# A gated linear attention with a sorted mixture of experts on one core: column tiles for the gate loop's small matmuls, and expert tiles of 128 tokens with all weights held in SBUF

## The chip, the core and the metric

The kernel runs on one core of one Trainium2 chip, in one launch. The metric is the device time of that launch in microseconds. The engines are named as the profile names them: PE (TensorE matmuls), PEld (TensorE weight loads), DVE (VectorE), ACT (ScalarE), POOL (GpSimd) and SP (SyncE). SP issues only DMAs here. A name with a q behind it (SPq, POOLq) is the sequencer or queue of that engine.

## The reference

There are two parts, and the first one's output is the input of the second. The first is a recurrence over 768 positions for 4 x 8 heads with a state of 48 x 48 complex numbers:

```
for t in range(S):                              # S = 768, B = 4, H = 8, D = 48
    new_re = ar * S_re - ai * S_im              # ar, ai: the gate of step t, cut to |a| <= 0.999
    new_im = ar * S_im + ai * S_re
    S_re, S_im = new_re + outer(k[t], v[t]), new_im
    y[t] = q[t] @ S_re
```

The second takes the rows of y, one row of 8 x 48 = 384 numbers for each of the N = 3072 tokens, and sends each token to the best of 8 experts:

```
logits = x @ w_gate + modality_bias[modality_id]      # x: (3072, 384), 8 experts
e_idx  = argmax(logits);  gate_w = softmax(logits)[e_idx]
out[mask_e] = gate_w * (relu(x[mask_e] @ w1[e]) @ w2[e])   # w1: (8, 384, 1024), w2: (8, 1024, 384)
```

All inputs and the output are float32.

## The kernel before

**Gate loop.** The recurrence is computed in blocks of L = 96 positions. The work is cut into two rounds of two batches each. For each round `elem(r)` does the elementwise part: it walks backwards over 12 chunks of 8 positions, normalises the gates (lines 64 to 81), forms running products of them on DVE (lines 84 and 85), scales q and k with them (lines 98 to 101), writes the scaled k to DRAM as `kh` (line 102), and turns the scaled q around on PE into the tile `QT` (lines 106 and 107). `A` and `QT` live in the pool `qt` with one buffer each, so the second round's `QT` can be written only when the first round's units have read theirs.

`units(r)` then does the matmuls: eight blocks g, and in each two batches b, so 16 units a round and 32 in all. A unit loads `KW` (the block's scaled k) and `V`, turns k around into `KT` (line 139, 140), multiplies it with `QT` into the 96 x 96 block `W` per head (line 145, in PSUM as `wp`), masks it into the second half of `KW` (line 146), turns the carried state `Z` around (line 150), and forms the new state and the output in one PSUM tile `py` (lines 160 and 164, in pairs of heads whose results lie on partitions 0 to 63 and 64 to 127). The output yT is copied twice (lines 170, 171); the float32 copy is multiplied with the gate weights `wgp` into the logits `lg_ps` (line 173: four accumulating matmuls with 8 columns of weights each), the bf16 copy is turned around and written to DRAM as the rows `x_rows` (lines 176 to 180). After both batches the logits of the block are turned around (line 185) and put into `lg`. In float32 a matmul that is no transpose shows up as two instructions in the profile.

**Routing.** `moe_sorted` opens its own pools once those of the gate loop are closed. DVE adds the bias, finds the best expert of each token, and counts tokens by expert (lines 258 to 308). Two small matmuls give ranks and counts, a scan gives each expert's first slot tile, and 32 float32 matmuls (line 344) build the list that says which token sits in which slot (`inv`, then `idg` for reading rows and `ids` for writing them).

**Experts.** Tokens sit in slot tiles of 256, each of which belongs to one expert. `cast_weights`, called ahead of the gate loop, has written bf16 copies of all weights to DRAM (`w1b`, `w2b`) through 16 casting DMAs on POOL's queue. `slot_tile(i)` reads the tile's expert into a register of SP, loads that expert's w1 and w2 from the bf16 copies (three buffers), gathers twice 128 rows by indirect DMA, turns them around (line 367), multiplies with w1 (line 375), applies relu on DVE and ACT by turns, multiplies with w2 (line 384), scales, and scatters twice 128 rows to the output by indirect DMA on POOL's queue (line 390). The first 12 slot tiles always run. The other 7 are nested conditionals; in the profiled execution one of them ran.

The order of the instructions on each engine is set by the framework's scheduler, which goes by program order and its own idea of when operands are ready; it also adds every semaphore wait, and gives a pool's place in SBUF to a later pool once its tiles have been read.

Of the kernel before, what the change touches and what calls it, by code (L numbers as in the profile page):

```python
# [22 lines left out]
def gate_loop(nc, ctx, tc, cpool, ident, identb, q, k, v, a_re, a_im, wgp, x_rows, lg):  # L23
# [3 lines left out]
    L = 96  # L27
# [18 lines left out]
    nc.gpsimd.affine_select(mask[:], mask[:], pattern=[[1, L]], compare_op=Alu.is_ge, fill=0.0, base=0, channel_multiplier=-1)  # L46

# [62 lines left out]
    def units(r):  # L110
# [4 lines left out]
        for g in range(G):  # L115
# [12 lines left out]
            lg_ps = ps.tile([8, NB, L], F32, name="lg_ps", tag="lg")  # L128
            for b in range(NB):
# [5 lines left out]
                KT = un.tile([C, H, L], F32, name="KT")  # L135
                for h4 in range(0, H, 4):
# [3 lines left out]
                    nc.scalar.copy(KT[:, h4:h4 + 4], tp[:])  # L140
                for h4 in range(0, H, 4):
                    wp = ps.tile([L, 4, L], F32, name="wp", bufs=2)
                    for i in range(4):
                        p = (b * H + h4 + i) * G + g
                        nc.tensor.matmul(wp[:, i, :], KT[:, h4 + i, :], QT[:, p, :], start=True, stop=True)  # L145
                    nc.vector.tensor_tensor(KW[:, h4:h4 + 4, C:], wp[:], mask[:, None, :].broadcast_to([L, 4, L]), Alu.mult)  # L146
# [25 lines left out]
                for j in range(J):  # L172
                    nc.tensor.matmul(lg_ps[:, b, :], wgp[:, j, :], yT[:, j, :], start=(j == 0), stop=(j == J - 1))  # L173
# [7 lines left out]
            lgT = un.tile([8, NB, L], F32, name="lgT")  # L181
            nc.scalar.copy(lgT[:], lg_ps[:])
            lp = ps.tile([L, NB, 8], F32, name="tl", tag="tp", bufs=2)
            for b in range(NB):
                nc.tensor.transpose(lp[:, b, :], lgT[:, b, :], ident[:8, :8])
# [11 lines left out]
def cast_weights(nc, moe_w1, moe_w2):  # L197

    E, Dt, F = moe_w1.shape
    w1b = nc.dram_tensor("w1b", (E, 128, Dt // 128, F), BF16, kind="Internal").ap()  # L200
    w2b = nc.dram_tensor("w2b", (E, 128, F // 128, Dt), BF16, kind="Internal").ap()
    for e in range(E):
        nc.gpsimd.dma_start(out=w1b[e], in_=moe_w1[e].rearrange("(k p) f -> p k f", p=128))
        nc.gpsimd.dma_start(out=w2b[e], in_=moe_w2[e].rearrange("(c p) d -> p c d", p=128))
    return w1b, w2b


def moe_sorted(nc, ctx, tc, cpool, identb, lg, x_rows, w1b, w2b, moe_modality_id, moe_modality_bias, out):

    N, Dt = out.shape  # L210
    E = w1b.shape[0]
    F = w1b.shape[3]
# [4 lines left out]
    SL = 256  # L217
    NL = N // SL
    NS = NL + E - 1
    HS = SL // 128  # L220
    NH = NS * HS
    NF = F // 128

# [3 lines left out]

# [243 lines left out]
```

## Time and profile before

| | |
|---|---|
| time, median of 3 runs | 740.69 us (739.15 to 748.84) |
| time of the profiled execution | 740.69 us |
| its span, first to last instruction | 739.0 us |
| mean granted TensorE clock | 0.80 |
| PE busy | 409.7 us (55%) |
| PEld busy | 307.4 us (42%) |
| DVE busy | 377.1 us (51%) |
| ACT busy | 268.0 us (36%) |
| POOL busy | 72.1 us (10%) |
| bytes moved by DMA | 91.42 MB |
| read from HBM, written to HBM | 86.75 MB, 29.59 MB |

Busy time is given over the whole span, and no engine is busy for much more than half of it, since the stages have different limits. The view of busy time by stretch therefore has to be read stage by stage. A matmul's mean duration is its latency; how often one starts is seen from the start times in the timeline. A wait is put down to the engine or transfer that ended last before the instruction began. The granted clock is the share of TensorE's full speed that was granted in a stretch.

### The profile page before, as it was taken

Reading aid. Unit: us, or ns where it says so; the run is one execution under the profiler, and the core shown is the slowest. Engines: PE = TensorE matmul, PEld = TensorE weight load, DVE = VectorE, ACT = ScalarE, POOL = GpSimd, SP = SyncE. Lnnn points to the kernel's source line nnn. Section 1 sums busy time; section 2 is a strip of 40 time slices with the busy share of each in tenths; the row PEclk is TensorE's granted clock in tenths of the full one; section 3 lists DMA queues with packets and bytes.
Section 4 is the critical chain, followed back from the end, with each engine's and each line's share of the span. In section 5 each row is a group of like instructions: output and inputs, shape, how many; then the busy total and the mean of one; then the engine's idle time right before and its main releaser. Section 6 shows DMA issues by size and latency. Waiting matters only on the chain. (4 is left out here: it accounts for less than half of the span.)

```text
span 739.0 us, 8928 instructions
## 1 busy us (share of the span) xinstructions
PE 409.7 (55%) x3112; PEld 307.4 (42%) x3112; DVE 377.1 (51%) x838; ACT 268.0 (36%) x597; POOL 72.1 (10%) x112
## 2 busy tenths in 40 slices
PE   0111112128988888921111789999993578686724
PEld 0101101016766666620110566777772556464412
DVE  3877777761276567787777023333335414232201
ACT  2545454532355446764544223334331002121100
POOL 4110000000000000000000000000000043344231
PEclk9999999999699679965555556879787559898866
DMA  9999923243346253243230433334201627676320
GB/s 208 235 249 244 259 65 128 64 132 93 82 101 166 55 142 78 60 156 122 64 107 30 112 73 79 78 79 95 57 21 6 256 72 280 231 252 221 131 64 4
DMA packets 107953, 91.42 MB, mean 124 GB/s; under 512 B 72894, under 2 KB 96866, under 8 KB 107904
## 3 DMA queue, kind: packets, MB, share of 16 engines
q1 hardware_dynamic: 28512, 51.27, 21.5%
q0 software_dynamic: 14432, 19.86, 12.9%
q10 hardware_dynamic: 64960, 19.67, 11.8%
q8 instruction: 26, 0.43, 0.2%
q14 instruction: 23, 0.19, 0.1%
HBM read 86.75 MB, written 29.59 MB: 157 GB/s over the span
## 5 line engine op out<-in xcount | busy, mean ns | idle before, releaser
L106 PE MATMUL tq<-ident,Qh 128*96 128x128 f32 x192 | 41.9, 392 | 218.3 <-DVE Qh L100 216.6
L106 PEld LDWEIGHTS tq<-ident,Qh 128*96 128x96 f32 x192 | 31.6, 181 | 227.8 <-ACT g L75 176.8
L146 DVE TENSOR_TENSOR KW<-wp,mask 96x384 f32<-96x384 f32 x64 | 35.1, 553 | 120.2 <-PE wp L145 119.1
L160 PE MATMUL py<-KW,V 96*64 96x192 f32 x512 | 81.6, 401 | 7.7 <-issue 6.1
L84 DVE TENSOR_TENSOR x<-A,an 128x192 f32<-128x192 f32 x192 | 68.6, 357 | 31.1 <-ACT an L81 25.4
L145 PE MATMUL wp<-QT,KT 96*96 96x96 f32 x512 | 70.8, 302 | 1.5 <-ACT KT L140 1.4
L145 PEld LDWEIGHTS wp<-QT,KT 96*96 96x96 f32 x512 | 62.9, 210 | 10.8 <-ACT Zs L152 4.5
L379 ACT ACTIVATE hT<-h_ps 128x512 bf16<-128x512 f32 x26 | 15.5, 597 | 130.4 <-PE h_ps L375 77.4
L93 ACT ACTIVATE sqe<-A 128x768 f32<-128x768 f32 x24 | 20.2, 843 | 96.3 <-DVE A L85 96.3
L133 POOL MEMSET V<- 96x128 f32 x32 | 6.4, 212 | 475.9 <-PE py L160 351.6
L85 DVE TENSOR_TENSOR A<-x 128x96 f32<-128x96 f32 x192 | 49.4, 257 | 6.4
L375 PE MATMUL h_ps<-xgT,w1t 128*128 128x256 bf16 x312 | 47.3, 321 | 5.8 <-DVE xgT L368 4.5
L160 PEld LDWEIGHTS py<-KW,V 96*64 96x64 f32 x512 | 40.2, 165 | 19.6 <-issue 14.9
L164 PE MATMUL py<-QT,Zs 96*48 96x96 f32 x448 | 48.2, 281 | 0.0
L139 PE MATMUL tk<-ident,KW 96*96 96x96 f32 x256 | 39.8, 297 | 11.8 <-DMA KW<-kh 10.6
L375 PEld LDWEIGHTS <-w1t 128*128 128x128 bf16 x312 | 35.8, 115 | 16.5 <-issue 7.6
L170 ACT COPY yT<-py 128x192 f32<-128x192 f32 x64 | 20.4, 319 | 61.2 <-DVE state L169 54.8
L107 ACT COPY QT<-tq 96x512 f32<-96x512 f32 x48 | 27.4, 583 | 33.8 <-PE tq L106 33.8
L173 PE MATMUL lg_ps<-yT,wgp 128*8 128x96 f32 x256 | 37.1, 276 | 4.4 <-ACT yT L170 3.2
L164 PEld LDWEIGHTS py<-QT,Zs 96*48 96x48 f32 x448 | 34.4, 142 | 10.9 <-ACT Zs L152 2.3
L140 ACT COPY KT<-tk 96x384 f32<-96x384 f32 x64 | 29.3, 476 | 21.8 <-DMA KW<-kh 11.2
L384 PE MATMUL y_ps<-w2t,hT 128*128 128x384 bf16 x208 | 36.3, 328 | 0.0
(115 smaller groups left out, 676.9 us busy)
## 6 DMA issues: line engine op xcount, KB each, us to landing
w1t<-w1b SPq DMA_DIRECT2D x13, 768.0 KB
w2t<-w2b SPq DMA_DIRECT2D x13, 768.0 KB
kh<-A SPq DMA_DIRECT2D x24, 384.0 KB
KW<-kh ACTq DMA_DIRECT2D x32, 288.0 KB
w1b<-in_moe_w_dram POOLq DMA_DIRECT2D x8, 768.0 KB
w2b<-in_moe_w_dram POOLq DMA_DIRECT2D x8, 768.0 KB, 42.0
cB<-c_scr ACTq DMA_DIRECT2D x28, 192.0 KB
ab<-in_a_re_dram SPq DMA_DIRECT2D x24, 192.0 KB
```

Of the source, the lines that this page charges most:

```text
L84: nc.vector.tensor_tensor(x[:], A[:, t + 1, :, None, :].broadcast_to([P, 2, 2, D]), an[:, t - t0].rearrange("p (u w) d -> p u w d", u=2), ...
L85: nc.vector.tensor_tensor(A[:, t], x[:, 0], x[:, 1], Alu.add)
L106: nc.tensor.transpose(tp[:, i, :], Qh[:, t4 + i].rearrange("p c d -> p (c d)"), ident[:])
L139: nc.tensor.transpose(tp[:, i, :], KW[:, h4 + i, 0:C], ident[:L, :L])
L140: nc.scalar.copy(KT[:, h4:h4 + 4], tp[:])
L145: nc.tensor.matmul(wp[:, i, :], KT[:, h4 + i, :], QT[:, p, :], start=True, stop=True)
L146: nc.vector.tensor_tensor(KW[:, h4:h4 + 4, C:], wp[:], mask[:, None, :].broadcast_to([L, 4, L]), Alu.mult)
L160: nc.tensor.matmul(py[u * 64:(u + 1) * 64, i, :], V[:, 2 * j + u, :], KW[:, 2 * j + u, :], start=True, stop=(g == 0))
L164: nc.tensor.matmul(py[u * 64:u * 64 + D, i, C:], Zs[:, j, u * 64:u * 64 + D], QT[:, p, :], start=False, stop=True)
L173: nc.tensor.matmul(lg_ps[:, b, :], wgp[:, j, :], yT[:, j, :], start=(j == 0), stop=(j == J - 1))
L375: nc.tensor.matmul(h_ps[:, f, :], w1t[:, k, ff * 128:(ff + 1) * 128], xgT[:, k, :], start=(k == 0), stop=(k == KD - 1))
L384: nc.tensor.matmul(y_ps[:], hT[:, f, s * 128:(s + 1) * 128], w2t[:, f, :], start=(f == 0), stop=(f == NF - 1))
```

## The change

Three things change.

1. In the gate loop, `W` is computed in two column tiles of 64 keys. `KT` is widened from 96 to 128 columns, the last 32 of which POOL sets to zero, and each head's matmul becomes two, with 64 columns of `KT` each, whose results lie on partitions 0 to 63 and 64 to 127 of `wp`.
2. Also there, the four logit matmuls of a unit no longer accumulate. Each writes its own column tile of 32 partitions (`wgp` is padded from 8 to 32 columns), and the four parts, which stand for the four pairs of heads, are summed afterwards by a matmul with `pairsum`, a 128 x 8 matrix of four stacked identities. This matmul takes the place of the transpose of the logits.
3. The bf16 copies of the weights in DRAM go. `w1s` and `w2s` in SBUF hold all eight experts' weights as bf16; they are filled by 16 casting DMAs on POOL's queue that stand at the start of `moe_sorted`, ahead of its iotas. The slot tiles have 128 tokens instead of 256, 31 of them run and none is conditional, and the tile's expert is read into a register of PE, which picks the weights inside `w1s` and `w2s` by it. The scatter's source `y_sb` comes from ACT alone.

The routing is the same but for the sizes: 32 columns of slots instead of 38, and the table of experts by tile is computed on all partitions.

```diff
@@ gate_loop
+    pairsum = cpool.tile([P, 8], F32, name="pairsum")
+    nc.vector.tensor_tensor(pairsum[:], ident[:, 0:8], ident[:, 32:40], Alu.add)
+    nc.vector.tensor_tensor(pairsum[:], pairsum[:], ident[:, 64:72], Alu.add)
+    nc.vector.tensor_tensor(pairsum[:], pairsum[:], ident[:, 96:104], Alu.add)
...
-            lg_ps = ps.tile([8, NB, L], F32, name="lg_ps", tag="lg")
+            lg_ps = ps.tile([P, NB, L], F32, name="lg_ps", tag="lg")
...
-                KT = un.tile([C, H, L], F32, name="KT")
+                KT = un.tile([C, H, P], F32, name="KT")
+                nc.gpsimd.memset(KT[:, :, L:], 0.0)
...
-                    nc.scalar.copy(KT[:, h4:h4 + 4], tp[:])
+                    nc.scalar.copy(KT[:, h4:h4 + 4, 0:L], tp[:])
                 for h4 in range(0, H, 4):
-                    wp = ps.tile([L, 4, L], F32, name="wp", bufs=2)
+                    wp = ps.tile([P, 4, L], F32, name="wp", bufs=2)
                     for i in range(4):
                         p = (b * H + h4 + i) * G + g
-                        nc.tensor.matmul(wp[:, i, :], KT[:, h4 + i, :], QT[:, p, :], start=True, stop=True)
-                    nc.vector.tensor_tensor(KW[:, h4:h4 + 4, C:], wp[:], mask[:, None, :].broadcast_to([L, 4, L]), Alu.mult)
+                        for u in range(2):
+                            nc.tensor.matmul(wp[u * 64:(u + 1) * 64, i, :], KT[:, h4 + i, u * 64:(u + 1) * 64], QT[:, p, :], start=True, stop=True)
+                    nc.vector.tensor_tensor(KW[:, h4:h4 + 4, C:], wp[0:L], mask[:, None, :].broadcast_to([L, 4, L]), Alu.mult)
...
-                    nc.tensor.matmul(lg_ps[:, b, :], wgp[:, j, :], yT[:, j, :], start=(j == 0), stop=(j == J - 1))
+                    nc.tensor.matmul(lg_ps[j * 32:(j + 1) * 32, b, :], wgp[:, j, :], yT[:, j, :], start=True, stop=True)
...
-                nc.tensor.transpose(lp[:, b, :], lgT[:, b, :], ident[:8, :8])
+                nc.tensor.matmul(lp[:, b, :], lgT[:, b, :], pairsum[:], start=True, stop=True)
@@ moe_sorted
+    w1s = mp.tile([128, E, KD, F], BF16, name="w1s")
+    w2s = mp.tile([128, E, NF, Dt], BF16, name="w2s")
     mb = mp.tile([TP, nM, E], F32, name="mb")
     mid = mp.tile([TP, NT, 2], I32, name="mid")
...
+    for e in range(E):
+        nc.gpsimd.dma_start(out=w1s[:, e], in_=moe_w1[e].rearrange("(k p) f -> p k f", p=128))
+        nc.gpsimd.dma_start(out=w2s[:, e], in_=moe_w2[e].rearrange("(c p) d -> p c d", p=128))
 
     io128 = mp.tile([128, 128], F32, name="io128")
     nc.gpsimd.iota(io128[:], ...)
...
+    for i in range(NS):                                  # NS = N // 128 + E - 1 = 31
+        xg = fp.tile([128, Dt], BF16, name="xg", bufs=4)
+        nc.gpsimd.indirect_dma_start(out=xg[:], out_offset=None, in_=x_rows_dram, in_offset=bass.IndirectOffsetOnAxis(ap=idg[:, i:i + 1], axis=0))
+        te = nc.values_load(texp[0:1, i:i + 1], engines=[ET.PE], min_val=0, max_val=E - 1, ...)
+        xg_ps = pp.tile([128, KD, 128], BF16, name="xg_ps", tag="rk")
+        for k in range(KD):
+            nc.tensor.transpose(xg_ps[:, k, :], xg[:, k * 128:(k + 1) * 128], identb[:])
+        xgT = fp.tile([128, KD, 128], BF16, name="xgT")
+        nc.vector.tensor_copy(xgT[:], xg_ps[:])
+        hT = fp.tile([128, NF, 128], BF16, name="hT", bufs=2)
+        for g in range(2):
+            h_ps = pp.tile([128, NF // 2, 128], F32, name="h_ps", tag="r", bufs=2)
+            for f in range(NF // 2):
+                ff = g * (NF // 2) + f
+                for k in range(KD):
+                    nc.tensor.matmul(h_ps[:, f, :], w1s[:, bass.ds(te, 1), k, ff * 128:(ff + 1) * 128], xgT[:, k, :], start=(k == 0), stop=(k == KD - 1))
+            gs = slice(g * (NF // 2), (g + 1) * (NF // 2))
+            if g == 0:
+                nc.vector.tensor_relu(hT[:, gs], h_ps[:])
+            else:
+                nc.scalar.activation(hT[:, gs], h_ps[:], Act.Relu)
+        y_ps = pp.tile([128, Dt], F32, name="y_ps", tag="y", bufs=2)
+        for f in range(NF):
+            nc.tensor.matmul(y_ps[:], hT[:, f, :], w2s[:, bass.ds(te, 1), f, :], start=(f == 0), stop=(f == NF - 1))
+        y_sb = fp.tile([128, Dt], F32, name="y_sb")
+        nc.scalar.activation(y_sb[:], y_ps[:], Act.Copy, scale=inv[:, 1, i:i + 1])
+        nc.gpsimd.indirect_dma_start(out=out, out_offset=bass.IndirectOffsetOnAxis(ap=ids[:, i:i + 1], axis=0), in_=y_sb[:], in_offset=None, bounds_check=N - 1, oob_is_err=False)
@@ the kernel's body
-    wgp = cpool.tile([128, H // 2, E], F32, name="wgp")
+    wgp = cpool.tile([128, H // 2, 32], F32, name="wgp")
...
-    w1b, w2b = cast_weights(nc, moe_w1, moe_w2)
```

## The prediction

> **What bounds the kernel now.** I first cut the span into stages, with the view of busy time by stretch, at the instants where the timeline changes line (columns: stretch, its length, then PE, PEld, DVE, ACT, POOL busy with instruction counts, granted clock, DMA share, GB/s).
>
> ```profile
> 0.00:165.00 165.00, 22.97 (x96) 17.44 (x96) 118.49 (x282) 74.37 (x135) 14.31 (x26) 1.00 0.78 176
> 165.00:305.00 140.00, 120.77 (x1068) 91.48 (x1068) 78.14 (x175) 67.26 (x176) 3.02 (x15) 0.85 0.41 99
> 305.00:408.00 103.00, 24.46 (x159) 18.32 (x156) 80.62 (x187) 51.40 (x100) 0.20 (x1) 0.57 0.30 94
> 408.00:558.00 150.00, 136.08 (x1116) 103.42 (x1116) 46.21 (x84) 50.12 (x142) 2.62 (x13) 0.74 0.30 72
> 558.00:599.00 41.00, 16.16 (x81) 14.88 (x80) 19.30 (x46) 1.79 (x6) 2.85 (x8) 0.55 0.35 120
> 599.00:739.00 140.00, 89.30 (x598) 61.89 (x598) 34.29 (x65) 23.07 (x39) 49.12 (x50) 0.82 0.49 165
> ```
>
> Stages one and three are the elementwise rounds, led by DVE; two and four are the units, led by PE (136 of 150 us in the fourth); the fifth is the routing, a DVE chain with one 14 us matmul series; the sixth is the experts. The change touches all but the third. Next I asked what each later stage waits for (the waits, by total, count, longest):
>
> ```profile
> POOL xg L364 <- DVE empty L350: 37.2, 1, 37.2
> POOL out_dram L390 <- DMA out_dram<-y_sb,ids: 36.3, 11, 5.6
> POOL io L235 <- PE py L164: 25.0, 1, 25.0
> ```
>
> The third line matters most: the first tile of the expert pools (io128) could be written only once the last matmul of the last unit had read QT. The expert pools lie where the gate loop's pools lay. The second says that each scatter waits for the scatter before it to land. Then the timeline of PE in a steady expert tile, and of POOL near the end where nothing but scatters is queued:
>
> ```profile
> 616.38 0.33 PE L367 MATMUL xg_ps<-identb,xg 128*128 128x128 bf16 x3
> 617.52 0.33 PE L367 MATMUL xg_ps<-identb,xg 128*128 128x128 bf16 x3 [0.81 <-DVE xgT L368]
> 618.30 2.78 PE L375 MATMUL h_ps<-xgT,w1t 128*128 128x256 bf16 x24 [0.45 <-DVE xgT L368]
> 620.91 2.76 PE L384 MATMUL y_ps<-w2t,hT 128*128 128x384 bf16 x16
> ...
> 707.25 0.97 POOL L390 DMA_INDIRECT out_dram<-y_sb,ids  x1 [2.36 <-issue]
> 710.57 0.97 POOL L390 DMA_INDIRECT out_dram<-y_sb,ids  x1 [2.35 <-issue]
> ```
>
> A tile of 256 slots takes 7.13 us of PE (616.38 to 623.51), and scatters follow at 3.32 us. Thirteen tiles ran; the thirteenth, behind the conditional, began 14 us late.
>
> **The change, part by part.** The sum is made against the profiled execution, span 739.0; the median of the runs shown is 740.7, so 1.7 is added at the end.
>
> *Weights (the largest term).* The early cast to DRAM goes, and with it the 26 loads on SP's queue. In its place 16 casting loads on POOL's queue fill w1s and w2s, 49,152 bytes a partition each. The gate pools hold A 37,248 and QT 49,152, then 46,080 (st) and about 64,000 (un), by the shapes: some 196,000 bytes, and the two new tiles span the places of A and QT. By the io128 row they wait for the last unit too. So a transfer that lay under stage one moves to the end of stage four, where only the routing can hide it. Its size: moe_w1 and moe_w2 are 25.2 MB in f32, 12.6 MB as bf16. In the DMA queues' view from 40 to 80 us:
>
> ```profile
> q0 software_dynamic: 5526, 5.87, 86.4%
> q1 hardware_dynamic: 2438, 4.11, 31.7%
> ```
>
> The casts (q0) wrote 5.87 MB in 40 us at 86.4% of the engines; alone at 100% that is 0.170 MB/us, 74 us for all. Counted by bytes read plus written (q0 5.87 + 11.74, q1 twice 4.11: 25.8 MB in 40 us, 0.65 MB/us) the 37.7 MB take 58, and the longest is the 88 us that they took beside q1 (issued from 1.45, no bytes after 90). I take 72, near the queue's own row. Since te chooses inside one tile, the first expert matmul waits for all eight parts of w1s, and the gathers stand behind the casts in q0.
>
> The routing hides below that, but not freely: io128, idp1 and pref are now behind the 16 issues on POOL, and the ninth issue waits for the first transfer:
>
> ```profile
> 11.04 0.70 POOL L203 DMA_DIRECT2D w1b<-in_moe_w_dram  x1 [2.60 <-DMA w1b<-in_moe_w_dram]
> 49.86 0.84 POOL L204 DMA_DIRECT2D w2b<-in_moe_w_dram  x1 [5.03 <-DMA w2b<-in_moe_w_dram]
> ```
>
> The last went out after 48 of 88 us, so here after some 39 of 72. cand needs pref; from cand (564.9) to the first gather (596.3) is 31 us: ready at 70, just inside the 72. A gather lands 2.6 us after issue, so the first transposes come 74 us after the last unit, not 41: **+33** (+20 to +50). The smaller edits of the routing (past on 128 partitions, 32 columns in place of 38) change single DVE instructions of 0.3 to 1.4 us and lie under the weights.
>
> *Expert tiles.* 31 tiles of 128 run, none conditional: 3968 slots where 13 x 256 = 3328 ran. Per tile on PE: transposes to first h matmul 0.78 (617.52 to 618.30, with DVE's copy). Then 24 h matmuls: three transposes of the same 128x128 shape take 0.33 with 0.22 for one, 0.055 each, so 1.3 at least; but each weight load now has an address from a register. No PE row shows that; SP's row for the register arithmetic of L358 is 37 ns, a semaphore instruction is 51 ns on PE's queue against 17 to 28 on SP's, and 32 loads and matmuls of y issue within 0.95 us, 30 ns each. With 60 ns for the pair and 0 to 130 ns for the arithmetic a matmul costs 0.055 to 0.19, 24 cost 1.3 to 4.6; I take 2.6, the rate of today's L375 (24 in 2.61), as the nearest in kind. Then 0.2 for ACT's 0.60 us relu, which half of y's matmuls cover, and 8 y matmuls at 2.60/16: 1.3. TENSOR_LOAD of te, 0.49 on PE's queue at L394, ran there while y's matmuls were still in the array: nothing, or 0.49 if that cover goes. Sum **4.9 us a tile**, bounds 3.6 and 7.4. ACT (0.60 + 0.58) and DVE (0.36 + 0.69) are below it, and the scatter chain, 3.32 with one gather of 1.0 inside its wait, is the floor. 31 x 4.9 = 152, and about 7 after the last tile (scatter issue, landing, end) give 159 where 140 stood: **+19**.
>
> A page speaks for a smaller term: the Trainium skill, "TensorE: Matmul & The Clock Gate", section "Back-to-back issue gap", gives about 81 ns for a weight load and matmul with 128 moving columns. No row here has that shape; the transposes' 55 ns are below it. By the page h would be 1.9, and the whole 21 us less.
>
> *Gate loop.* Stage one: the first ab load landed at 8.45 because the casts shared the engines; alone, by the gathers' 2.6 us landing, near 5: -3.5. Chunks then follow at 12.5 us (Qh at 22.1, 34.6, ... 97.2, 109.8) with and without casts, so nothing more. Units: logits are 8 matmuls a unit at 0.43 per four; in column tiles the nearest row is L164, which already runs in pairs with the same 96 moving columns:
>
> ```profile
> 549.25 0.37 PE L164 MATMUL py<-QT,Zs 96*48 96x96 f32 x4
> 549.45 0.49 PE L160 MATMUL py<-KW,V 96*64 96x192 f32 x4
> ...
> 557.95 0.50 PE L173 MATMUL lg_ps<-yT,wgp 128*8 128x96 f32 x4
> 558.38 0.31 PE L176 MATMUL xp<-identb,yTb 128*96 128x128 bf16 x2
> ```
>
> Four take 0.20, so 0.86 falls to 0.40: -15 over 32 units. wp: 16 in 1.44 now (546.48 to 547.92); 32 with 64 weight columns at L164's 0.05 are 1.6, at L160's 0.08 2.6: +5 to +36; I take the nearer in columns moved, +5. The pair sums use the full 128 rows and two passes, +0.2 sixteen times: +3. Stage three begins when the units release QT and stage four is PE, so the units' gain passes on whole: **-10** with the start (-20 to +25). The 32 extra memsets of KT (0.2 us for half the elements at L133) lie in POOL's idle time; at worst the next u=1 matmul waits 0.4.
>
> The Trainium skill, "TensorEngine Tiling (Array Packing)", section "Key Properties", speaks against this part: changing the tiling mode drains the array, and W now adds changes in each unit. It gives no price, and no row here separates one; it could only raise the sum.
>
> **Sum.** 739 - 10 + 33 + 19 + 1.7 = **783**.
>
> **The rivals.** *Tiles near the floor:* PE's register work is cheap or later transposes fill the gaps, 3.6 us a tile: 783 - 31 x 1.3 = 743, no difference. For it: 55 ns transposes; against: 32 addresses a tile and today's 0.8 us bubble. *Sequencer or clock:* PE's queue needs two register steps a matmul, or the clock, 0.5 to 1.0 within today's units though PE is busy, stays down: 6.5 us a tile, 833. *Weights early:* the new tiles wait only for A, whose last reader is at 407 us, and load under the fourth stage. The io128 row speaks against it. That takes the 33 off: 750 at 4.9 us a tile, and it becomes faster than before by over 2% where a tile takes under 4.1; at 3.6, 710.
>
> **How the numbers follow.** The forecast (weights late, 4.1 to 6 us a tile) gets 0.60, tiles near the floor 0.15, sequencer or clock 0.15, weights early 0.10. The predicted time is the first's. The range reaches to the second's 743 and the third's 833: 742 to 832. Two per cent, about what a measurement of this kernel tells from no change, is 726 to 755. Faster: half of weights early and a sliver of the floor, 0.06; same: the rest of those with little over, 0.14; slower: 0.80.
>
> **What would show it.** q0 writing 12.6 MB, some 175 GB/s, for about 72 us from the last unit on, POOL's io128 about 40 us late, the first transposes 70 to 80 us after the last py; then 31 periods of 4 to 6 us with PE, not the scatter wait, setting them; PE time of the units within 10 us of now. It is wrong if w1s loads before 500 us, if the casts take under 50 us, or if a tile takes under 3.6 us or over 7.

## The result, and the profile after

The changed kernel takes 920.38 us (median of 4 runs, 912.18 to 939.99) where the kernel before took 744.77 beside it (median of 4): a ratio of 1.232, 95% interval 1.216 to 1.249. The forecast said slower, 783 us, with a range up to 832. The direction was right and the size far off. The profiled execution took 923.07 us, with a span of 921.0. Here and below, a ratio with an interval is made without the executions that were slowed by a lower clock, and a median is over all executions.

The stages were cut at the same events in both traces: the first matmul that turns the scaled k around, the end of the first round of units, the first of the second round, its end, the first transposes of gathered rows, the end. The view of busy time by stretch, kernel before (columns: stretch, length, then PE, PEld, DVE, ACT and POOL busy with instruction counts, granted clock, DMA share, GB/s):

```profile
168.40:310.70 142.30, 126.31 (x1127) 95.45 (x1127) 82.48 (x186) 70.27 (x185) 3.22 (x16) 0.86 0.39 96
310.70:413.30 102.60, 19.07 (x98) 14.34 (x99) 76.12 (x174) 48.98 (x92) 0.00 (x0) 0.55 0.32 99
413.30:559.60 146.30, 137.37 (x1128) 104.28 (x1128) 46.84 (x89) 50.53 (x145) 3.39 (x18) 0.75 0.28 67
559.60:599.10 39.50, 14.71 (x68) 13.99 (x69) 18.67 (x41) 0.80 (x3) 2.17 (x3) 0.54 0.36 125
599.10:739.00 139.90, 89.30 (x598) 61.89 (x598) 34.29 (x65) 23.07 (x39) 49.02 (x50) 0.82 0.49 165
```

The same view of the changed kernel:

```profile
167.80:329.00 161.20, 149.81 (x1400) 112.49 (x1401) 79.84 (x174) 69.97 (x183) 8.14 (x32) 0.73 0.35 81
329.00:439.30 110.30, 22.20 (x98) 16.61 (x99) 79.76 (x185) 50.26 (x93) 0.00 (x0) 0.52 0.33 97
439.30:567.50 128.20, 118.89 (x1400) 90.17 (x1400) 46.21 (x84) 50.86 (x145) 6.93 (x27) 0.87 0.37 76
567.50:639.40 71.90, 14.73 (x70) 14.04 (x70) 19.73 (x46) 0.64 (x3) 16.27 (x24) 0.52 1.07 178
639.40:921.00 281.60, 256.53 (x1085) 121.19 (x1085) 32.54 (x62) 36.49 (x62) 59.11 (x60) 0.62 0.09 28
```

Read down the second column. The stage of routing and weights grew by 32.4 us, the gate loop by 8 (its end moved from 559.6 to 567.5), nearly all of it in the elementwise round between the two rounds of units (102.6 to 110.3). The experts doubled, from 139.9 to 281.6. Of the 182 us by which the span grew, 142 are there, where the forecast had 19. In that last row PE is busy for 256.5 of 281.6 us, so it is PE that is slow; the waits for DMA in it are 0.3 us in all (DMA share 0.09), and the clock is only 0.62.

The timeline of PE in a steady tile of the changed kernel shows which instructions (start, length, engine, line, operation, tiles, shape, count):

```profile
711.58 5.56 PE L372 MATMUL h_ps<-xgT,w1s 128*128 128x128 bf16 x24 [0.45 <-DVE xgT L365]
716.93 0.42 PE L363 MATMUL xg_ps<-identb,xg 128*128 128x128 bf16 x2
717.15 2.76 PE L380 MATMUL y_ps<-w2s,hT 128*128 x8
719.71 0.31 PE L363 MATMUL xg_ps<-identb,xg 128*128 128x128 bf16 x1
720.47 1.66 PE L372 MATMUL h_ps<-xgT,w1s 128*128 128x128 bf16 x7 [0.45 <-DVE xgT L365]
```

From one h series to the next, 711.58 to 720.47, is 8.9 us. The 24 h matmuls take 5.35 us (to 716.93; 5.4 in most tiles), or 0.225 each, and the eight y matmuls 2.56 (717.15 to 719.71). Lengths in the second column overlap the next group, so starts are compared. Then the groups of line 372, which this time hold what PE's queue did for them, and those of line 380 (columns: line, engine, operation, count, shortest/median/longest in ns, then the first and last start in us). PEldq is PE's queue, and FUSED_REGOPS is a register step, which works out an address:

```profile
L372 PEldq FUSED_REGOPS  x1488: 46/55/60, 640.6 to 912.0; - x186
L372 PEld LDWEIGHTS <-w1s x744: 95/103/152, 640.8 to 912.0; 128*128 x186
L372 PE MATMUL h_ps<-xgT,w1s x744: 216/263/266, 641.0 to 912.1; 128*128 128x128 bf16 x186
```

```profile
L380 PEldq FUSED_REGOPS  x248: 51/55/55, 646.4 to 913.6; - x124
```

There are 1488 register steps for 744 h matmuls: two for each, one ahead of its weight load and one ahead of the matmul itself, 55 ns each. So an h matmul is four entries on PE's queue, and 225 / 4 = 56 ns an entry. The trace shows them one after the other: in most pairs, 8 ns after a matmul has started the next register step starts, 105 ns after that the weight load, 8 ns later the second step, and 105 ns after that the matmul. That is 113 ns for either half, so the matmul's address costs as much as the weight load's. In y only the moving operand has an address from the register: 248 steps for 248 matmuls.

The waits (engine, tile, line, what it waited for: total, count, longest in us) name the same series, and no longer the scatters:

```profile
ACT hT L377 <- PE h_ps L372: 235.2, 31, 66.6
...
DVE cand L279 <- POOL pref L239: 24.8, 1, 24.8
```

ACT's relu waits for h in each of the 31 tiles. The second line belongs to the routing: its chain waited once, 24.8 us, for an iota that stands behind the casting loads on POOL.

### The profile page after: what moved, and what is told of

Same layout as the page of the kernel before. It is cut to its first block, busy times and chain, and to the rows that moved or that the text cites. A ratio compares the mean times of both kernels' runs of the same rounds, so it can differ in the third digit from the quotient of the medians.

```text
span 921.0 us, 12780 instructions
## 1 busy us (share of the span) xinstructions
PE 585.1 (64%) x4143; PEld 371.8 (40%) x4143; DVE 377.3 (41%) x838; ACT 282.6 (31%) x620; POOL 92.3 (10%) x154
## 5 line engine op out<-in xcount | busy, mean ns | idle before, releaser
L372 PE MATMUL h_ps<-xgT,w1s 128*128 128x128 bf16 x744 | 169.3, 250 | 19.1 <-DVE xgT L365 14.6
L372 PEld LDWEIGHTS <-w1s 128*128 x744 | 76.5, 103 | 116.5 <-issue 41.1
L380 PE MATMUL y_ps<-w2s,hT 128*128 x248 | 83.8, 516 | 0.0
L153 PE MATMUL wp<-QT,KT 96*64 96x96 f32 x1024 | 74.3, 311 | 3.0 <-ACT KT L147 1.4
L365 DVE COPY xgT<-xg_ps 128x384 bf16<-128x384 bf16 x31 | 11.1, 358 | 148.6 <-PE xg_ps L363 148.6
L153 PEld LDWEIGHTS wp<-QT,KT 96*64 96x64 f32 x1024 | 64.0, 181 | 12.2 <-ACT KT L147 9.3
L375 DVE TENSOR_SCALAR hT<-h_ps 128x512 bf16<-128x512 f32 x31 | 21.4, 692 | 92.6 <-PE h_ps L372 92.6
L142 POOL MEMSET KT<- 96x256 f32 x32 | 9.8, 307 | 455.6 <-PE wp L153 455.6
L359 POOL DMA_INDIRECT xg<-x_rows,idg x31 | 30.1, 972 | 203.4 <-PE xg_ps L363 171.4
L380 PEld LDWEIGHTS <-hT 128*128 128x128 bf16 x248 | 35.5, 148 | 31.8 <-issue 31.3
```

The lines of the kernel that those rows point to most:

```text
L153: nc.tensor.matmul(wp[u * 64:(u + 1) * 64, i, :], KT[:, h4 + i, u * 64:(u + 1) * 64], QT[:, p, :], start=True, stop=True)
L359: nc.gpsimd.indirect_dma_start(out=xg[:], out_offset=None, in_=x_rows_dram, in_offset=bass.IndirectOffsetOnAxis(ap=idg[:, i:i + 1], axis=0))
L372: nc.tensor.matmul(h_ps[:, f, :], w1s[:, bass.ds(te, 1), k, ff * 128:(ff + 1) * 128], xgT[:, k, :], start=(k == 0), stop=(k == KD - 1))
L375: nc.vector.tensor_relu(hT[:, gs], h_ps[:])
L380: nc.tensor.matmul(y_ps[:], hT[:, f, :], w2s[:, bass.ds(te, 1), f, :], start=(f == 0), stop=(f == NF - 1))
```

## Experiments on the expert tiles

A time without an interval is that of a single execution, with its profile.

**No addresses from a register.** The first question was whether the register steps are the whole of it, or the shape of the tiles, or the clock. Every tile takes expert 0's weights here; the choice of the expert is left out, and with it the read of the expert's number into PE's register.

```diff
-        te = nc.values_load(texp[0:1, i:i + 1], engines=[ET.PE], ...)
...
-                    nc.tensor.matmul(h_ps[:, f, :], w1s[:, bass.ds(te, 1), k, ...
+                    nc.tensor.matmul(h_ps[:, f, :], w1s[:, 0:1, k, ...
...
-            nc.tensor.matmul(y_ps[:], hT[:, f, :], w2s[:, bass.ds(te, 1), f, :], ...
+            nc.tensor.matmul(y_ps[:], hT[:, f, :], w2s[:, 0:1, f, :], ...
```

> The changed kernel with the weights of expert 0 in every slot tile, so no address from a register (this leaves the choice of the expert out). Theory (PE's sequencer): each of the 24 h matmuls of a tile costs four instructions of some 57 ns on PE's queue, two of them register arithmetic, together 230 ns, while the array needs 53 to 107 ns; the idle array keeps the clock near 0.6 and doubles y as well. Without the arithmetic h falls from 5.6 to 1.3 to 2.6 us a tile, the clock rises above 0.8, y falls from 2.6 to 1.4, a tile takes 4 to 5 us where it took 9.0, and the span is 770 to 810. Rival (the clock by itself): the clock stays near 0.6, h is 2.6 and y 2.6, a tile 6.3, span about 840. Rival (small tiles, their waits): a tile stays above 8 us, span above 890.

It took 767.43 us, 156 less than the profiled execution of the changed kernel and 2.6 below the low end of what was expected. The transposes began at 637.4 (639.4 in the changed kernel), and the tiles took 128 us instead of 282. PE's timeline:

```profile
702.18 1.50 PE L371 MATMUL h_ps<-xgT,w1s 128*128 128x128 bf16 x24 [0.45 <-DVE xgT L364]
703.52 0.28 PE L362 MATMUL xg_ps<-identb,xg 128*128 128x128 bf16 x2
703.86 1.47 PE L379 MATMUL y_ps<-w2s,hT 128*128 128x384 bf16 x8
705.17 0.22 PE L362 MATMUL xg_ps<-identb,xg 128*128 128x128 bf16 x1
705.84 1.50 PE L371 MATMUL h_ps<-xgT,w1s 128*128 128x128 bf16 x24 [0.45 <-DVE xgT L364]
```

```profile
640.00:760.00 120.00, 100.69 (x1068) 70.31 (x1066) 32.00 (x61) 36.52 (x62) 56.22 (x57) 0.99 0.21 64
```

The 24 h matmuls go from 5.4 to 1.34 us (702.18 to 703.52), which is 56 ns each; a tile takes 3.66 us here and 3.9 in the median. So an address from the register costs (225 - 56) / 2 = 85 ns for each instruction that carries it, of which the row of its register step accounts for 55; no row shows what fills the rest. And the clock goes from 0.62 to 0.99: y's eight matmuls, whose array work is the same, fall from 0.32 us each in the changed kernel to 0.16. So the register steps cost twice: on the queue in h, and by the low clock in y. What shows that the clock follows is only that the two came and went together, in this run and the next ones.

The Trainium skill, "TensorE: Matmul & The Clock Gate", section "Back-to-back issue gap", gives about 81 ns for a stream of weight loads and matmuls with 128 moving columns, and about 56 for the isolated gap. This run's stream of such pairs ran at 56 ns, so here the smaller figure held for the stream; and the 225 ns of the changed kernel are on no line of that section.

**Register addresses for w2 alone.** The next run tells h's share from y's; the choice of the expert is left out of w1.

```diff
-                    nc.tensor.matmul(h_ps[:, f, :], w1s[:, bass.ds(te, 1), k, ...
+                    nc.tensor.matmul(h_ps[:, f, :], w1s[:, 0:1, k, ...
```

> The changed kernel with expert 0's w1 in every tile but w2 still picked by the register (this leaves half of the choice of the expert out). Theory (PE's sequencer): y has one register instruction a matmul, three instructions of 57 ns or 175 ns, against 160 ns in the array at full clock, so its arithmetic is nearly hidden: the span is within 10 us of the kernel with both fixed. Rival (every register address costs alike): 8 of 32 addresses a tile remain, a quarter of what the fixed kernel saved comes back, some 30 us.

784.92 us. Of the 17 us above the run before, 8 lie ahead of the tiles, which began at 645.7 here. The tiles took 137 us, 9 more than without any register address, with the clock at 0.97. PE's timeline:

```profile
704.31 1.46 PE L380 MATMUL y_ps<-w2s,hT 128*128 x8 [0.56 <-DVE hT L375]
705.61 0.22 PE L363 MATMUL xg_ps<-identb,xg 128*128 128x128 bf16 x1
```

The eight y matmuls with their register steps start every 0.16 us, as without them. What is new is an idle 0.56 us ahead of them in each tile, and the trace shows what stands there: the read of the expert's number on PE's queue (TENSOR_LOAD, 703.81 to 704.11), then y's first register step (704.21). In the changed kernel the same read lies beside y's matmuls. So y's matmuls lose nothing to their addresses, and this wait is enough for the 9 us. The register addresses of w1 are worth the other 145 of the 154 us. The expectation of 10 us for the whole span was missed (17), and met by the tiles.

**The same matmuls with 256 columns.** If the price is one of instructions, it is the same for twice the columns. The h matmuls keep their register addresses; h, relu and y are cut up as in the kernel before.

```diff
-    NS = N // 128 + E - 1
+    NS = N // 256 + E - 1
...
-        xgT = fp.tile([128, KD, 128], BF16, name="xgT")
+        xgT = fp.tile([128, KD, 256], BF16, name="xgT", bufs=2)
```

> The changed kernel with slot tiles of 256 tokens, 19 of them, none conditional; weights stay in SBUF and are picked by PE's register. Theory (PE's sequencer, a cost for each matmul): 24 h matmuls at 230 ns are 5.5 us a tile whatever their columns, y 16 times 0.175 to 0.32, transposes 1.9: 10.2 to 12.5 us a tile, 19 tiles 194 to 238 in place of 282, span 833 to 877, and the clock is above 0.62 since the array is busy for longer of each 230 ns. Rival (a cost for each column): two times 9.0 a tile, 19 tiles 342, span about 980.

843.53 us. PE's timeline in a steady tile:

```profile
692.78 5.71 PE L374 MATMUL h_ps<-xgT,w1s 128*128 128x256 bf16 x24 [0.55 <-DVE xgT L367]
698.35 2.76 PE L383 MATMUL y_ps<-w2s,hT 128*128 x16
700.94 0.33 PE L366 MATMUL xg_ps<-identb,xg 128*128 128x128 bf16 x3
```

The 24 h matmuls take 5.57 us again, with twice the columns and at a clock of 0.99 (660 to 800 us). This is the run that parts queue and clock: the clock was full, and the h series still took what it took at 0.62. So the clock has no part in h; the queue sets it. In y, with its register steps and at the full clock, 16 matmuls take what 8 took in the changed kernel, so there it is the clock and not the steps. The array was busy for about half of the h series here and for a quarter in the changed kernel, an estimate from the 56 ns for 128 columns at fixed addresses (24 x 2 x 56 ns of 5.57 us, 24 x 56 ns of 5.4).

**w1 as the moving operand.** If the number of register instructions sets the time, a tile that needs few should run like one without any, and still do the whole work. Six matmuls of 512 columns with w1 moving take the place of 24 with w1 as weights; h then comes out token by token and has to be turned around by eight transposes.

```diff
+        for g in range(2):
+            h_ps = pp.tile([128, F // 2], F32, name="h_ps", tag="r", bufs=2)
+            gs = slice(g * (F // 2), (g + 1) * (F // 2))
+            for k in range(KD):
+                nc.tensor.matmul(h_ps[:], xgT[:, k, :], w1s[:, bass.ds(te, 1), k, gs], start=(k == 0), stop=(k == KD - 1))
...
+            for f in range(NF // 2):
+                nc.tensor.transpose(ht_ps[:, f, :], hb[:, ff * 128:(ff + 1) * 128], identb[:])
```

> The changed kernel with the operands of the first expert matmul exchanged: xgT stands still and 512 columns of w1s, picked by the register, move past it, 6 matmuls of h a tile in place of 24; h then comes out by rows and is turned around by 8 bf16 transposes. Theory (each instruction with a register address costs PE's queue two slots of some 57 ns): 14 register instructions a tile in place of 56, so h is bound by the array, 6 x 0.21 = 1.3 us, the transposes add 0.5 and one more wait for DVE or ACT, the clock stays above 0.9: 4.5 to 6 us a tile in place of 9.0, span 785 to 830. Rival (weights picked by a register at run time are slow in themselves, by where they lie): h stays near 5 us, span above 880.

770.89 us, 14 below the low end of what was expected. PE's timeline, one period:

```profile
654.82 1.24 PE L371 MATMUL h_ps<-w1s,xgT 128*128 x5
655.90 0.33 PE L363 MATMUL xg_ps<-identb,xg 128*128 128x128 bf16 x3
656.26 0.94 PE L381 MATMUL ht_ps<-identb,hb 128*128 128x128 bf16 x8
657.31 0.38 PE L371 MATMUL h_ps<-w1s,xgT 128*128 x1
657.53 1.46 PE L389 MATMUL y_ps<-w2s,hT 128*128 x8
658.82 1.24 PE L371 MATMUL h_ps<-w1s,xgT 128*128 x5
```

A tile takes 4.00 us with 14 register steps instead of 56, at a clock of 0.97, though it has eight transposes more. The count of instructions with register addresses, and not the choice of weights in SBUF by a register, is what the changed kernel pays for.

## Experiments on the weights

**The iotas ahead of the loads.** The forecast had the routing and the casts end within 2 us of each other. To see whether the routing's late start mattered, the 16 casting loads were moved behind the iotas (number ramps that the routing needs) on POOL.

```diff
-    for e in range(E):
-        nc.gpsimd.dma_start(out=w1s[:, e], ...)
-        nc.gpsimd.dma_start(out=w2s[:, e], ...)
     nc.gpsimd.iota(io128[:], ...)
...
     nc.gpsimd.iota(thr[:], ...)
+    for e in range(E):
+        nc.gpsimd.dma_start(out=w1s[:, e], ...)
+        nc.gpsimd.dma_start(out=w2s[:, e], ...)
```

> The changed kernel with the iotas of the routing ahead of the 16 casting loads on POOL's queue. Theory (the casts end at 634 and the routing at 636.5, so both set the start of the tiles): the routing now ends some 35 us earlier, the casts alone set the start, the first transposes come 2 to 5 us earlier (from 73 us after the last unit's last py to 68 to 72) and the span changes by no more than that. Rival (the routing held behind POOL's issues is what sets the start): the first transposes come 30 us earlier.

916.0 us. PE's timeline from the routing to the first transposes:

```profile
590.55 13.88 PE L348 MATMUL inv_ps<-load,onlo 96*128 96x64 f32 x64 [14.24 <-DVE load L345]
631.89 0.50 PE L364 MATMUL xg_ps<-identb,xg 128*128 128x128 bf16 x3 [27.46 <-DMA xg<-x_rows,idg]
```

The routing was over some 30 us earlier, and PE then waited 27.46 us for the first gather, behind the casts in the same queue. The transposes came 69 us after the last unit instead of 73.5. So the loads by themselves need that long, and the order of the issues is worth some 5 us.

**Copies made early, loads by SP.** Then the other side: the bf16 copies of the kernel before, written ahead of the gate loop, and SP loading them into w1s and w2s after it.

```diff
+    w1b, w2b = cast_weights(nc, moe_w1, moe_w2)          # ahead of the gate loop, as before
...
-        nc.gpsimd.dma_start(out=w1s[:, e], in_=moe_w1[e]...)
-        nc.gpsimd.dma_start(out=w2s[:, e], in_=moe_w2[e]...)
+        nc.sync.dma_start(out=w1s[:, e], in_=w1b[e])
+        nc.sync.dma_start(out=w2s[:, e], in_=w2b[e])
```

> The changed kernel with the weights cast to bf16 copies in DRAM at the start, as before, and loaded into w1s and w2s by SP's queue once the gate loop's pools are free. Theory (the exposed cast is the 33 us of the start): 12.6 MB instead of 25.2 are read, POOL's queue is free at once, so the first transposes come 40 to 45 us after the last unit's last py instead of 73, and the span falls by 28 to 33. Rival (any load of all experts' weights at that place is exposed): 12.6 MB into SBUF takes 60 us or more, and the gain is under 15.

902.17 us. The first transposes came 45 us after the last unit (576.3 to 621.3), where the kernel before, with no weights to wait for, had 41, so some 28 of the 33 us were gone. The total fell by only 21, where 28 to 33 were expected, since this run's gate loop ended 11 us later than the changed kernel's. The DMA queues' view from 578 to 620 us:

```profile
q1 hardware_dynamic: 5616, 12.69, 79.1%
```

(Columns: queue, packets, MB, share of 16 engines.) At this view's rate of 400 to 430 GB/s in most slices the 12.6 MB took 30 us. The changed kernel's casts, read from the same view from 569 to 640 us, wrote at about 205 GB/s in most slices and took 64:

```profile
q0 software_dynamic: 11585, 12.76, 105.4%
```

The Trainium skill, "DMA: Bandwidth & Descriptors", section "Measured (HBM→SBUF, 128 partitions, SWDGE, issued from GpSimd)", lists 425 GB/s for the largest transfer. The loads of bf16 copies here agree with it, though they are on SP's queue and not POOL's; the casts agree only if the bytes read are counted (25.2 MB in 64 us is 393 GB/s), which that section doesn't say.

## Experiments on the gate loop

The forecast took 10 us off the gate loop; it grew by 8. Three kernels put its two edits on the kernel before, together and apart, with the routing and the experts left as they were before.

```diff
@@ W: KT widened to 128 columns, two matmuls of 64 columns a head
+                        for u in range(2):
+                            nc.tensor.matmul(wp[u * 64:(u + 1) * 64, i, :], KT[:, h4 + i, u * 64:(u + 1) * 64], QT[:, p, :], ...)
@@ logits: wgp padded to 32 columns, four column tiles, summed by pairsum
+                    nc.tensor.matmul(lg_ps[j * 32:(j + 1) * 32, b, :], wgp[:, j, :], yT[:, j, :], start=True, stop=True)
```

Both edits:

> The kernel before with both changes of the gate loop alone (W and logits in column tiles, the pair sums by a matmul); experts and weights as before. In the changed kernel the second round's units took 128 us where they took 146, at a higher clock, and the first round's 161 where they took 142, at a lower one. Theory (the column tiles save PE time as predicted, the clock of a run moves both rounds by more than that): 5 to 15 us less than the kernel before, 726 to 738. Rival (the column tiles lower the granted clock and cost time): the first round is again near 160 at a clock near 0.7, total 750 to 760. Rival (a change of DVE's order in the first round costs what PE gains): 739 to 747, with fewer chunks of the second elementwise round done by the time the units end.

W alone:

> The kernel before with W in two column tiles alone. Theory: 32 matmuls in 1.54 us where 16 took 1.44 at full clock, +3 us of PE over 32 units, and 32 memsets on POOL that hide: within 5 us of the kernel before. Rival (the changes of tiling mode cost): 10 us or more slower.

Logits alone:

> The kernel before with the logits in four column tiles and the pair sums by a matmul, alone. Theory: four logit matmuls take 0.29 us where they took 0.43, less 9 us of PE over 32 units, the pair sums add 0.2 sixteen times, +3: 3 to 10 us faster. Rival (the shorter matmuls only leave PE waiting for ACT's copies of yT and lgT): within 3 us of the kernel before.

| edit | median | ratio to before, 95% |
|---|---|---|
| both | 750.42 (10 runs) | 1.009, 1.001 to 1.018 |
| W in column tiles | 731.38 (4 runs) | 0.977, 0.964 to 0.990 |
| logits in column tiles | 767.72 (4 runs) | 1.030, 1.020 to 1.040 |

None of the three came out as its theory had it, and the signs are the wrong way round: W, for which 5 us were added, gains some 17, and the logits, for which 15 were taken off, cost some 22. The matmuls themselves are not to blame. This is PE's timeline of the changed kernel at the end of the last unit:

```profile
561.26 1.54 PE L153 MATMUL wp<-QT,KT 96*64 96x96 f32 x32 [0.57 <-ACT KT L147]
...
565.87 0.36 PE L181 MATMUL lg_ps<-yT,wgp 128*32 128x96 f32 x4
566.16 0.31 PE L184 MATMUL xp<-identb,yTb 128*96 128x128 bf16 x2
```

From start to start, the 32 W matmuls take 1.47 us (to the next group at 562.73) where 16 took 1.44; four logit matmuls take 0.29 where they took 0.43; the clock was 1.00 in these stretches of both traces. By these, W costs 1 us in 32 units and the logits give 9.

The time went elsewhere. Here are the elementwise round between the two rounds of units and the second round of units, with W alone:

```profile
312.20:415.90 103.70, 19.05 (x99) 14.33 (x100) 74.57 (x168) 47.71 (x90) 0.00 (x0) 0.55 0.33 100
415.90:550.80 134.90, 125.97 (x1384) 95.37 (x1384) 46.84 (x89) 50.58 (x145) 7.70 (x32) 0.83 0.32 72
```

And with the logits alone:

```profile
324.60:440.90 116.30, 20.68 (x101) 15.57 (x101) 83.85 (x194) 53.87 (x101) 0.00 (x0) 0.53 0.32 92
440.90:587.70 146.80, 138.21 (x1144) 105.38 (x1144) 46.83 (x89) 50.76 (x145) 3.40 (x18) 0.72 0.31 66
```

In the elementwise round DVE has 168 instructions left with W alone, 174 before, 185 in the changed kernel, 186 with both edits and 194 with the logits alone, and the round lasts 103.7, 102.6, 110.3, 109.6 and 116.3 us. DVE's order is fixed when the kernel is built, and an edit of PE's work alters how many steps of `elem(1)` the scheduler puts between the units of the first round; what it doesn't put there is done later, on the path. That accounts for 14 of the 29 us between the profiled executions of before and of the logits alone. The count does not vary from one execution to the next: between the last masking of `KW` in the first round and the first in the second, DVE has 189 instructions in all eight profiles with both edits, and the round lasts 109 to 110 us in each; in the four with W alone in the gate loop they are 174 and 103 to 104. The count is a rough measure (W alone has six fewer left than before, and a round 1 us longer), and the order was not changed by itself in any run: that it sets the length is argued and not tested.

The rest is in the start and in the units (the first round took 154 us at a clock of 0.81, where before had 142 at 0.86), and there the granted clock differs with it. W alone ran its second round in 134.9 us at 0.83, where before had 146.3 at 0.75. But the same gate loop code had a first round of 161 us at 0.73 and a second of 128 at 0.87 in the changed kernel, and 140 at 0.83 and 142 at 0.76 with both edits on the kernel before. The changed kernel and the five variants of it that leave the gate loop and the casts' place behind it alone show the spread: a first round from 140.6 us (0.84) to 161.2 (0.73), a second from 128.2 (0.87) to 148.4 (0.72), and an end of the gate loop from 563 to 574 us. Why the clock goes one way or the other in a stage in which PE is busy nine tenths of the time stays open, and with it why W alone gains. A round's length goes with the clock by up to 20 us, more than either edit.

## Towards a faster kernel

**W tiles and a second PSUM buffer.** With W alone ahead, an idle step in its expert tiles was tried: the transposes of a tile's second half wait 0.8 us for the copy of the first, since `xg_ps` has one buffer.

```diff
-            xg_ps = pp.tile([128, KD, 128], BF16, name="xg_ps", tag="rk")
+            xg_ps = pp.tile([128, KD, 128], BF16, name="xg_ps", tag="rk", bufs=2)
```

> The kernel before with W in two column tiles and the experts' xg_ps in two PSUM banks instead of one, so that PE need not wait 0.81 us in the middle of each tile of 256 for DVE's copy. Theory: 10 us less than with W's tiles alone (13 tiles of 0.8), 715 to 725. Rival (the scatters, 3.32 us each and two a tile beside two gathers, are the next bound at 6.6 to 7.1 us a tile): 0 to 5 us less than with W's tiles alone, 726 to 732.

743.68 us (10 runs), a ratio of 1.003, interval 0.997 to 1.009: slower than W alone, where both expectations had it at least as fast. From the waits of this kernel:

```profile
DVE y_sb L391 <- DMA out_dram<-y_sb,ids: 39.2, 6, 8.7
```

With W alone this wait was 17.5 to 25.1 us in two profiles. The transposes now run back to back, and the time comes back as a wait of `y_sb` for the scatters, which follow each other at their own pace. So the idle step of PE was not on the path. The whole is slower than W alone, measured beside it, by some 12 us: 7 are in the expert stage (147.2 us, where W alone had 140.5 and 140.0), and the rest is in the gate loop, whose code is the same and which ended at 552.7 where W alone had 550.8 and 545.1.

**W tiles again.** The gain of W was repeated on another chip.

> The kernel before with W in two column tiles alone, once more, on this chip and beside the other: 0.977 of the kernel before in the first comparison (0.964 to 0.990). If that came from the column tiles it is 0.965 to 0.99 again; if it was the clock of that hour it is 0.99 to 1.01.

731.85 us (5 runs), a ratio of 0.985, interval 0.970 to 0.999. A gain is there again, somewhere between nothing and 4% by the two intervals together; this one reaches into the rival's 0.99.

**All that spoke for itself.** Last, W tiles, logits as before, early copies loaded by SP, and expert tiles with w1 moving.

```diff
     # the changed kernel, with
+    w1b, w2b = cast_weights(nc, moe_w1, moe_w2)                                    # ahead of the gate loop
+        nc.sync.dma_start(out=w1s[:, e], in_=w1b[e])                               # and w2s from w2b
+                    nc.tensor.matmul(lg_ps[:, b, :], wgp[:, j, :], yT[:, j, :], start=(j == 0), stop=(j == J - 1))
+                nc.tensor.matmul(h_ps[:], xgT[:, k, :], w1s[:, bass.ds(te, 1), k, gs], ...)   # w1 moving
```

> Put together from the parts that the runs so far speak for: W in column tiles as in the change; logits as before (four accumulating matmuls of 8 columns); the bf16 copies of the weights written to DRAM ahead of the gate loop as before and loaded into w1s and w2s by 16 DMAs on SP's queue once the last unit is done; expert tiles of 128 with w1 as the moving operand. Sum from their rows: the last unit at about 545 us (as with W tiles alone), 44 us to the first transposes (as with the copies alone), 31 tiles of 4.0 us (as with w1 moving), 7 behind the last, 1.7 around the span: 722, a ratio to before of 0.965 to 0.985, some 9 us below W tiles alone. Rival: the clock or the loads of SP's queue cost it again what the experts give (loads beside the first gathers, a longer gate loop because fewer steps of elem(1) lie in the shadow of the first round's units): 735 to 755, a ratio of 0.99 to 1.02; then the stage to look at is the one between the two rounds of units.

731.94 us (10 runs), a ratio of 0.987, interval 0.982 to 0.992. It beats the changed kernel and, by one to two per cent, the kernel before, and falls short of the sum by 10 us. Its tiles are as expected, by the view of busy time by stretch:

```profile
598.00:729.70 131.70, 115.98 (x760) 63.75 (x775) 45.68 (x93) 54.65 (x93) 58.90 (x60) 0.95 0.20 60
```

From the first transposes to the first scatter are 12 us, then 30 periods of 3.8 and 5 to the end; the first transposes came 45 us after the last unit (553.4 to 598.0). Both are within a microsecond of the terms (31 x 4.0 + 7 = 131; 44). What missed is the gate loop, whose last unit ended at 553.4 and not 545. That term was the better of two profiles of W alone; the other ended at 551. So weights in SBUF are worth about 8 us in the expert stage (131.7 against 139.9 before), cost about 4 ahead of it (45 against 41 from the last unit to the first transposes), and no more than W tiles alone comes of the whole.

## Why the prediction was wrong, step by step

The span missed its forecast by 140 us: the experts took 123 more than their term, the gate loop 18, and the weights what was forecast.

**The failed step: the size of the term for the h matmuls.** The mechanism was named (an address from a register for each weight load), and so was the place (PE's queue). The forecast counted one register step for each matmul, let it cost 0 to 130 ns, and took the rate of the matmuls of before, 0.109 us each and 2.6 for 24; its upper bound was 0.19. Measured: 0.225, since the matmul instruction has a register step of its own as well, and either half takes the queue 113 ns. The trace of before had the rows for it: a semaphore instruction took 51 ns on PE's queue. Two steps of that length beside two instructions at the same price would have given 0.2 us and a tile of 7 us or more. The forecast read that row, but priced the weight load with its matmul at 60 ns as a pair, from y's pairs, whose 32 entries had no register step and were issued within 0.95 us.

**What followed from it and was not in the sum.** At 0.225 us a matmul the array works for about a quarter of the time, by the 56 ns of the run without register addresses, and the clock came down to about 0.6, so that y took 2.6 us a tile where 1.3 was forecast. A tile missed by 4.0 us (8.9 against 4.9), of which h holds 2.8 and y 1.3. The rival named for this, sequencer or clock, had them as alternatives at 6.5 us a tile and 833 us. Both came true at once, and 8.9 lies above the upper bound of 7.4 as well.

**The experts' other terms held.** Without the register addresses a tile takes 3.66 to 3.9 us, and the low bound was 3.6. The forecast said that no row had a weight load with 128 moving columns; the transposes of before are that, at 55 ns, and the h matmuls at fixed addresses took 56. TENSOR_LOAD took 300 ns on PE's queue and lay in the shadow of y, as forecast; with h short and y on register addresses it came out of that shadow.

**The weights: right.** +33 was forecast and +32.4 measured; the first transposes came 73.5 us after the last unit (565.9 to 639.4) and 74 was forecast. The casts were taken as 72 us and took 64; the routing was taken as ready 70 after the last unit and the first gather was issued after 70.8 (565.9 to 636.7). From the timeline of POOL:

```profile
569.81 0.95 POOL L230 DMA_DIRECT2D w1s<-in_moe_w_dram  x1 [21.30 <-DVE seg L241]
...
604.22 0.90 POOL L231 DMA_DIRECT2D w2s<-in_moe_w_dram  x1 [3.13 <-DMA w2s<-in_moe_w_dram]
605.12 0.26 POOL L235 IOTA io<- 128x128 f32 x1
...
636.67 1.03 POOL L359 DMA_INDIRECT xg<-x_rows,idg  x1 [30.74 <-DVE empty L353]
```

That the sum came out to the microsecond is partly luck: the casts ended at about 634, 8 us sooner than forecast, and the routing, held back by the issues, set the start instead. The first cast is issued only after the last unit, the last one 34 us later, and io128 behind it: each as forecast. The rival with early weights is refuted by the first line.

**The gate loop: wrong, -10 against +8.** The terms of the matmuls were near (W +5 against 1, logits -15 against -9), and the start's 3.5 us came to 0.6 (168.4 to 167.8); with the gate loop's two edits but the early casts kept the units began at 171, so the casts were worth some 3 and the edits cost most of it again. What failed is the step that the units' gain passes on whole. The forecast left the third stage untouched, and that stage grew by 7.7 us, while the two rounds of units together stayed as they were (288.6 and 289.4). The trace of before showed both reasons against the step: a third stage led by DVE, whose length depends on what was done beside the units, and two rounds of the same units at clocks of 0.85 and 0.74. That interval of -20 to +25 held the outcome.

## What to carry to other kernels

A register in a matmul's operand is paid on PE's queue, once for each instruction that carries it, so count the instructions and not the bytes: put the chosen operand where there are few of them (long moving operands), and keep the short ones at fixed addresses. Price an instruction that the trace doesn't show by the nearest entry of the same queue, and add every such entry up, before taking a rate from instructions that were hidden. And where a static order or a clock ties stages together, a saving of a microsecond on one engine can be outweighed by what the scheduler then does with another; put each edit alone on the kernel before.

## What the runs showed of the hardware

- A register-addressed weight load and matmul, each with a register step of 55 ns on PE's queue, took 0.225 to 0.232 us together, for 128 columns (clock 0.62) and for 256 (clock 0.99) alike; the same pair at fixed addresses started every 56 ns.
- The granted clock did not go by PE's busy time: it was 0.62 with PE busy 91% of the expert stage by the profile, and 0.99 for the same tiles without register addresses, where PE was busy 84%. In these runs it went with the array's share of the time (0.62 with the array busy for a quarter of the h series, 0.99 for a half, by the estimate above). In the gate loop it was anywhere from 0.72 to 0.87 for the same code.
- Casting DMAs from f32 to bf16, with next to no other transfer beside them, wrote 12.6 MB in 64 us; loading the finished bf16 copies took 30 us.
- Two matmuls in column tiles of 64 cost as much as one of 96: 32 in 1.47 us, 16 in 1.44, at a clock of 1.00 both times. No price of a change of tiles is visible there.
